# Tile 0 of a fused attention and MLP kernel: two hidden blocks in unsplit float32, normalised rows from the third on, and another order of the first stage

## The chip, the cores and the metric

The kernel runs on one core of one Trainium2 chip. The metric is device time in microseconds (us) of one execution, of which several are taken. Besides, one execution was recorded by the hardware profiler; all durations below come from that one.

The engines are named as in the profile: PE multiplies matrices (PEld loads its weights), DVE is the vector engine, ACT the scalar engine, POOL is GpSimd, and SP only issues DMAs here.

## What is computed

Linear attention with a decay, then an RMS norm with a gated MLP, then a second MLP:

```python
state = alpha[:, :, t, :, None] * state + np.einsum('bhd,bhe->bhde', k[:, :, t], v[:, :, t])
y[:, :, t] = np.einsum('bhd,bhde->bhe', q[:, :, t], state)
...
xn = x / rms * rms_g                    # x: 3072 tokens x 384, rms over the 384
g, val = xn @ w_gate, xn @ w_val        # 384 x 1536 each
x = (g / (1 + exp(-g)) * val) @ w_out   # 1536 x 384
...
h = x @ w_in                            # 384 x 2048
out = (h * cos(h)) @ w_out2             # 2048 x 384
```

All data is float32. There are 4 batches of 8 heads of width 48, over 768 positions.

## The kernel before

**Tiles and units.** The 3072 tokens are 8 tiles of 384 (half a batch each). The attention of a tile is four units, one for a pair of heads: unit 0 to 3 belong to tile 0, unit 4 to 7 to tile 1, and so on; u8 below is the first of tile 2. Features lie on the partitions, tokens along a row.

**A unit** goes through these steps. `att_prep` (L340): DVE scans the decay along the tokens (L347), takes a reciprocal and a second scan (L349), multiplies q (L359) and k (L356). `att_T` (L386): PE transposes k (`pt`), ACT copies it (`th`, L394). `att_sc0` (L424): PE forms the scores (`ps`), ACT copies them and POOL sets the part above the diagonal to zero (`sm`, L398 and L399). `att_u` (L440): PE multiplies k by v (`pu`), DVE scales it (`w`, L454) and adds up the states (L458); what goes on to the next tile is the carry `c`. `att_y` (L474): PE adds scores times v and states times q (`py`), and the sum is copied into the tile's rows `xT`, for tile 0 one half by ACT (L502) and one by DVE (L503). The first unit of a tile holds the pair of heads whose rows fill the 16 spare partitions of the three row blocks, so six small DMAs on SP (`att_fix`, L505: 16 rows each, two to a block) move them there.

**The first MLP** has 12 hidden blocks f of 128. For each: `m1_gate` (L740) forms `pg`, multiplies it by 1/rms (L747, for tiles below NRAW = 3; DVE) and takes Silu on ACT (`th`, L749); `m1_val` (L754) forms `pv`, multiplies it by `th` (L762) and splits the product into `hh` and `hl`; `m1_unit` (L766) adds its three products to the accumulators `o`. After block 11 `o` is scaled, for tile 0 to 2 by 1/rms as well (L779). A float32 matrix is used as the sum of two float32r parts, high and low; `mm9` (L699) multiplies high by high, high by low, low by high: three passes for each block of 128 rows, so nine for `pg` and `pv` and nine for the three `o`.

**The weights** come as float32 seen as 64-bit integers, in pieces of 128 by 768. `assemble` (L183) turns a staged piece (`st_g`, `st_v`, `st_o`; `ws` for later, smaller ones) into floats: the low word on ACT (L186), the high word on ACT (L188), both joined on DVE (`cv`, L189). `split` (L193) makes the two float32r parts: a copy on ACT (L86) and a subtraction on DVE (L89).

**The norm of tile 0.** `x_split` (L598) scales the rows by the norm's weights `g_sb` and splits them; `square` (L516) squares `xT` in three pieces; `rms_rows` (L538) sums them by 12 matmuls; `rms_inv` (L548) finds the inverse root by nine small DVE operations, the last of which spreads it out (`yb`); `rms_out` (L570) turns it into a tile `y0` of all 128 rows by one matmul (`rb`) and an ACT copy (L578).

**Order.** For tile 0 the string FIRST (L48) lists the pieces in the order in which they are issued, and `in_order()` keeps each engine to it: p, T, s, u, y are the steps of a unit, a and b the two halves of a weight's conversion, x, q, r, n, o the norm, g, v, P the first gate and value blocks, S the staging of weights, and i fills PE's time with that many matmuls on ones (`keep_clock`, L531). From there on the pieces of the next tile's attention, and the remaining conversions (steps in CONV, L52), are streamed in by `slot()` (L1038) between the MLP's matmuls; a scheduler in the compiler places the rest. Each engine runs its instructions in that order and waits at the first one that is not ready. SP issues all loads, in one queue, in the order of its list.

Of the kernel before, what the change touches and what calls it, by code (L numbers as in the profile page):

```python
# [55 lines left out]
def fused_kernel(ctx: ExitStack, tc: tile.TileContext, akq, vin, wg, wv, wo, g_in, w2i, w2o, out):  # L56
# [18 lines left out]
    sd = []  # L75

    def make_bd():
        for i in range(1):
            bd.append([at.tile([R, NB, 2, C], F32R, name=f"bd{x}{i}") for x in "hl"])
# [19 lines left out]
    mean = const.tile([128, 128], F32, name="mean")  # L99
    d1 = const.tile([R, NB, C + 1], F32, name="d1")  # L100
# [81 lines left out]

    def assemble(st, v):  # L183
        w = st.bitcast(I32).rearrange("p (n t) -> p n t", t=2)
        lo, hi = w[:, :, 0], w[:, :, 1]
        act.activation(out=lo, in_=lo.bitcast(U32), func=AF.Identity, scale=LOW_SCALE, bias=low)  # L186
        g = hi.bitcast(F32)
        done("act", act.activation(out=g, in_=g, func=AF.Prelu, scale=HIGH_SCALE, alpha=NEG_SCALE))  # L188
# [11 lines left out]
    half = []  # L200

    def conv_a():
# [4 lines left out]
        v = cv_tile(st)  # L207
        assemble(st, v)
        half.append((h, l, v))
        if tag and tag != "ws":  # L210
            free.append(tag)

    def conv_b():
        if half:
            h, l, v = half.pop(0)
            split(h, l, v.bitcast(F32))

# [122 lines left out]
    def att_prep(u):  # L340
        s = un[u]
        a, q = s["a"], s["q"]
        G = at.tile([R, NB, C + 1], F32, tag="G", name="G")
        n = NB * (C + 1)
        Gf = G.rearrange("p n c -> p (n c)")
        Iv = a[:, 1:n + 1]
        dve.tensor_tensor_scan(Gf, a[:, 0:n], d1.rearrange("p n c -> p (n c)"), 0.0, ALU.mult, ALU.add)  # L347
        dve.reciprocal(dr[:, :, C:C + 1], G[:, :, C:C + 1])
        dve.tensor_tensor_scan(  # L349
            Iv[:, ::-1], Iv[:, ::-1], dr.rearrange("p n c -> p (n c)")[:, ::-1],  # L350
            0.0, ALU.mult, ALU.add,
        )
# [86 lines left out]

    def att_u(u):  # L440
# [11 lines left out]
        w = at.tile([R, NB, D], F32, tag="w", bufs=2, name="w")  # L452
# [21 lines left out]
    def att_y(u):  # L474
# [63 lines left out]
    def rms_rows(i, c, n):  # L538
        if i not in rsum:
            rsum[i] = ps_a.tile([128, 512], F32, tag="a", name="rm")  # L540
        x = rms[i][c]
        for j in range(4):
            done("pe", pe.matmul(
                rsum[i][32 * j:32 * j + 32, :TQ], ones[:, :32], x[:, j * TQ:(j + 1) * TQ],
                start=c == 0, stop=c == n - 1,
            ))

    def rms_inv(i):  # L548
        ps = rsum.pop(i)
        m, y, t = (m1.tile([128, TQ], F32, tag="n" + x, name="n" + x) for x in "myt")  # L550
        done("act", act.activation(out=m, in_=ps[:, :TQ], func=AF.Identity, scale=1.0 / DM, bias=eps))
# [29 lines left out]
    def rms_wide(i):  # L581
# [3 lines left out]
        y = at.tile([128, TT], F32, tag="y2", name="y2") if i == 2 else m1.tile([128, TT], F32, tag="y", name="y")  # L585
        t = at.tile([128, TT], F32, tag="nt", name="nt")
# [5 lines left out]
        dve.tensor_tensor(out=t, in0=y, in1=y, op=ALU.mult)  # L592
        dve.tensor_tensor(out=t, in0=t, in1=m, op=ALU.mult)
        for o, s, x, z in (a, ROOT[1], t, t), (y, ROOT[2], a, y), (t, ROOT[3], t, t), (y, ROOT[4], t, y):
            done("dve", dve.scalar_tensor_tensor(out=o, in0=x, scalar=s, in1=z, op0=ALU.add, op1=ALU.mult))
        rms[i] = y

    def x_split(c, i=0):  # L598
        if c == 0:
            xn[i] = tuple(m1.tile([128, 3, TT], F32R, tag="x" + k, name="x" + k) for k in "hl")  # L600
        x, (xh, xl), g = xT[i][:, c, :], xn[i], g_sb[:, c:c + 1]
        ah = act.activation(out=xh[:, c, :], in_=x, func=AF.Copy, scale=g)
        ad = dve.scalar_tensor_tensor(
            out=xl[:, c, :], in0=x, scalar=g, in1=xh[:, c, :].bitcast(F32), op0=ALU.mult, op1=ALU.subtract
        )
        if i == 0:
            done("act", ah)
            done("dve", ad)
# [15 lines left out]
    def att_pieces(i):  # L624
        u0 = 4 * i

        def y(u):
# [4 lines left out]
            if i == 0 and u == u0:  # L632
                att_fix(i)
# [5 lines left out]
        if i == 0:  # L639
            def stage_rest(n):  # L640
# [5 lines left out]
                x=x_split, q=lambda c: square(0, c), r=lambda c: rms_rows(0, c, 3), i=lambda n: keep_clock(n, ones), l=load_all, S=stage_rest, P=lambda f: post.append(m1_gate(0, f)),  # L646
# [52 lines left out]
    def mm9(dst, w, rhs, first, last, cols, mm=pe.matmul):  # L699
        k = 0  # L700
        for kc in range(len(rhs)):
            for a, b in ((0, 0), (0, 1), (1, 0)):
                mm(  # L703
                    dst, w[a][:, cols(kc)], rhs[kc][b],
                    start=first and k == 0, stop=last and k == 3 * len(rhs) - 1,
                )
                k += 1
# [32 lines left out]
    def m1_gate(i, f):  # L740
# [5 lines left out]
        if i < NRAW:  # L746
# [7 lines left out]
    def m1_val(i, f, t):  # L754
# [5 lines left out]
        hh = m1.tile([128, TT], F32R, tag="hh", bufs=3, name="hh")  # L760
        hl = m1.tile([128, TT], F32R, tag="hl", bufs=3, name="hl")
# [4 lines left out]
    def m1_unit(i, f, j, mm=None):  # L766
        g, c = divmod(f, 4)
        if j == 0 and f == 0:
            acc1[i] = [ps_o.tile([128, 512], F32, tag=f"o{n}", name=f"o{n}") for n in range(3)]
        w = wt[f"o{g}"][0]  # L770
        h = hid1[i, f]
        k = slice(c * DM + j * 128, c * DM + j * 128 + 128)
        mm9(acc1[i][j][:, :TT], w, [h], f == 0, f == 11, lambda kc: k, mm or pe.matmul)
        if f == 11:
# [3 lines left out]
            if i < NRAW:  # L778
# [215 lines left out]

    dve.memset(d1, 0.0)
# [3 lines left out]
    dve.memset(eps, EPS)  # L999
# [38 lines left out]
    def slot():  # L1038
# [31 lines left out]
    for i in range(NTILE):  # L1070
# [7 lines left out]
        for f in range(12):  # L1078
# [5 lines left out]
            if f == 0 and 1 <= i < NRAW:  # L1084
                for x in range(2):
                    pre["g", x] = m1_mm(i, "g", x, ps_g.tile([128, 512], F32, tag="g", name="pg"))
                    late.pop(0)()
                    if x == 0:
                        pre["v", 0] = m1_mm(i, "v", 0, ps_g.tile([128, 512], F32, tag="g", name="pv"))
# [119 lines left out]
```

## Time and profile before

| | before |
|---|---|
| median of 3 runs | 994.01 us (993.57 to 994.18) |
| the profiled execution, own time | 995.94 us |
| its span (first to last recorded instruction) | 994.2 us |
| PE busy | 977.3 us, 98% |
| DVE, ACT, POOL busy | 709.5, 608.5, 118.1 us |
| mean granted clock of TensorE | 0.997 of full speed |

The span of the profiled execution is 1.74 us shorter than its own time, and that time is 1.93 us over the median of the runs. A granted clock of 1.00 stands for TensorE's upper level (2.4 GHz), 0.50 for the lower one (1.2 GHz). A row of a timeline that ends in brackets tells how long the engine was idle before it, and which instruction ended the wait.

### The profile page before, as it was taken

The numbers are of one execution on the slowest core, as the hardware profiler recorded it, in microseconds if no ns is written. First come the engines' busy times: TensorE is split into PE (matmuls) and PEld (weight loads), VectorE is DVE, ScalarE is ACT, GpSimd is POOL, SyncE is SP. The second block draws the span as 40 slices with busy tenths as digits, with TensorE's granted clock in tenths as the row PEclk, the third lists the DMA queues.
The fourth block names the chain that finished last, engine by engine and source line by source line (L and its number), as shares of the span: only waits on it lengthen the run. The fifth ranks groups of instructions, "written<-read, shape, count | busy, mean of one in ns | idle before, by whom it ended". The sixth has DMA issues, their size and how long they took to land.

```text
span 994.2 us, 16986 instructions
## 1 busy us (share of the span) xinstructions
PE 977.3 (98%) x6451; PEld 900.9 (91%) x6451; DVE 709.5 (71%) x1333; ACT 608.5 (61%) x1270; POOL 118.1 (12%) x154
## 2 busy tenths in 40 slices
PE   8899999999999999999999999999999999999998
PEld 6698899999999999999999998888888888888886
DVE  7898778978877678578637227777767777777666
ACT  4878455565564565465633227777777677777764
POOL 3010011100110010010102211121201201211000
PEclk9999999999999999999999999999999999999999
DMA  7936334443453443544202575001010010000000
GB/s 232 323 103 193 98 91 128 138 130 96 139 155 101 139 126 102 146 137 126 89 18 88 199 304 170 19 26 39 1 43 22 1 54 12 32 1 1 33 1 32
DMA packets 44273, 96.71 MB, mean 97 GB/s; under 512 B 5520, under 2 KB 25488, under 8 KB 44192
## 3 DMA queue, kind: packets, MB, share of 16 engines
q1 hardware_dynamic: 41312, 79.90, 26.1%
q0 software_dynamic: 2880, 15.73, 4.3%
q8 instruction: 51, 0.84, 0.4%
q14 instruction: 30, 0.25, 0.1%
HBM read 69.26 MB, written 25.17 MB: 95 GB/s over the span
## 4 chain that ended last, share of the span: by engine, by line
PE 91%; DVE 5%; DMA 2%; ACT 1%; issue 1%; POOL 0%; SPq 0%; DVEq 0%; ACTq 0%; POOLq 0%
PE p L841 20%; PE pg L703 14%; PE pv L703 13%; PE o L703 13%; PE px L841 9%; PE py L841 9%; PE py L481 2%; PE pe L841 2%; PE py L486 2%; PE pu L448 1%; DMA ak<-akq 1%; PE ps L382 1%; PE pt L392 1%; PE ps L383 1%; PE ps L384 1%
## 5 line engine op out<-in xcount | busy, mean ns | idle before, releaser
L841 DVE SCALAR_TENSOR_TENSOR kk<-kk,c 128x512 f32<-128x512 int32 x192 | 148.5, 773 | 93.2 <-ACT kk L841 93.2
L841 PE MATMUL p<-hh,p 128*128 128x512 f32 x576 | 211.4, 396 | 0.2 <-ACT kk L841 0.2
L841 PEld LDWEIGHTS p<-hh,p 128*128 128x128 f32 x576 | 108.6, 189 | 17.2 <-ACT kk L841 0.3
L841 ACT ACTIVATE kk<-kk 128x512 f32<-128x512 f32 x192 | 115.7, 626 | 3.0
L841 PE MATMUL p<-hl,p 128*128 128x512 f32 x288 | 113.6, 394 | 0.2 <-DVE hl L89 0.2
L841 PE MATMUL px<-xh,i 128*128 128x256 f32 x481 | 113.8, 291 | 0.0
L841 PE MATMUL py<-xh,i 128*128 128x256 f32 x482 | 109.4, 282 | 0.0
L399 POOL TENSOR_SCALAR_AFFINE_SELECT sm<-sm 128x512 f32<-128x512 f32 (+1 forms) x64 | 46.5, 730 | 455.3 <-ACT sm L398 455.3
L762 DVE TENSOR_TENSOR pv<-th,pv 128x384 f32<-128x384 f32 x96 | 53.3, 556 | 63.3 <-PE pv L703 53.7
L841 PEld LDWEIGHTS px<-xh,i 128*128 128x128 f32 x481 | 84.1, 188 | 12.3 <-ACT py L841 12.3
L86 ACT ACTIVATE hh<-pv 128x384 fp32r<-128x384 f32 x96 | 46.8, 488 | 74.8 <-DVE pv L762 72.7
L841 PEld LDWEIGHTS py<-xh,i 128*128 128x128 f32 x482 | 84.2, 189 | 4.4 <-DVE hl L89 0.3
L749 ACT ACTIVATE th<-pg 128x384 f32<-128x384 f32 x96 | 46.7, 487 | 66.4 <-PE pg L703 45.2
L89 DVE TENSOR_TENSOR hl<-kk,hh 128x512 fp32r<-128x512 f32 x96 | 68.2, 710 | 3.3
L841 PE MATMUL px<-xl,i 128*128 128x256 f32 x240 | 67.8, 283 | 0.0
L841 PE MATMUL py<-xl,i 128*128 128x256 f32 x240 | 67.5, 281 | 0.0
L89 DVE TENSOR_TENSOR hl<-pv,hh 128x384 fp32r<-128x384 f32 x96 | 53.1, 553 | 19.3 <-ACT hh L86 18.3
L841 ACT ACTIVATE kk<-c 128x512 int32<-128x512 f32 x96 | 60.3, 628 | 1.6
L841 PEld LDWEIGHTS p<-hl,p 128*128 128x128 f32 x288 | 54.4, 189 | 5.6 <-DVE hl L89 1.0
L841 ACT ACTIVATE m<-pe 128x256 f32<-128x256 f32 x48 | 18.4, 384 | 53.8 <-PE pe L841 53.8
L841 PEld LDWEIGHTS py<-xl,i 128*128 128x128 f32 x240 | 45.2, 188 | 4.3
L841 ACT ACTIVATE c<-px 128x512 f32<-128x512 f32 x48 | 28.8, 599 | 31.8 <-PE px L841 31.6
(233 smaller groups left out, 2625.8 us busy)
## 6 DMA issues: line engine op xcount, KB each, us to landing
ak<-akq SPq DMA_DIRECT2D x29, 337.8 KB, 3.7
i<-d_i POOLq DMA_DIRECT2D x12, 768.0 KB, 5.9
ws<-w2i SPq DMA_DIRECT2D x16, 384.0 KB, 3.6
ws<-w2o SPq DMA_DIRECT2D x16, 384.0 KB, 3.6
d_p<-whl SPq DMA_DIRECT2D x32, 192.0 KB, 3.0
p<-d_p POOLq DMA_DIRECT2D x8, 768.0 KB, 6.4
v<-vin SPq DMA_DIRECT2D x32, 168.0 KB, 3.0
q<-akq SPq DMA_DIRECT2D x30, 168.0 KB, 2.9
```

The source lines that it names most:

```text
L86: return act.activation(out=dst, in_=src, func=AF.Copy)
L89: return eng.tensor_tensor(out=dst, in0=a, in1=h.bitcast(F32), op=ALU.subtract)
L382: pe.matmul(dst, a[0], b[0], start=start, stop=False)
L383: pe.matmul(dst, a[0], b[1], start=False, stop=False)
L384: pe.matmul(dst, a[1], b[0], start=False, stop=stop)
L399: pool.affine_select(out=dst, in_=dst, pattern=[[0, n], [1, C]], compare_op=ALU.is_ge, fill=0.0, base=0, channel_multiplier=-1,)
L481: pe.matmul(py[r0:r1, c], s["v"][:, n, r0:r1], s["s"][:, n, j, :], start=n == 0, stop=False)
L486: done("pe", pe.matmul(py[:R, c], sd[0][:, n, :], s["q"][:, c], start=False, stop=n == NB - 1))
L703: mm(dst, w[a][:, cols(kc)], rhs[kc][b], start=first and k == 0, stop=last and k == 3 * len(rhs) - 1,)
L749: done("act", act.activation(out=t, in_=p, func=AF.Silu, scale=1.0 / WS))
L762: dve.tensor_tensor(out=p, in0=t, in1=p, op=ALU.mult)
L841: last2[eng] = fn(*args, **kw).ins
```

## The change

The change touches tile 0, the start of tile 1 and the loads ahead of them.

- Hidden blocks 0 and 1 of tile 0 use the weights before they are split ("whole"), against the rows before the norm: three float32 matmuls where nine float32r ones stood, for `pg`, for `pv` and for `o`. `pg` and `pv` are then multiplied by `y0`. The splits of these three pieces are made later (steps 9, 11 and 13 of the stream). From block 2 on, tile 0 uses rows already multiplied by `y0` (`x_norm`), so neither its `pg` nor its `o` is multiplied by it.
- The rows are scaled by `g_sb` when they are copied out of PSUM (for the first unit by `g3`, its own piece of these weights, loaded by six DMAs of 16 values on ACT's queue); the squares are taken from PSUM, unit by unit, so that there are four pieces and 16 matmuls to sum them. For units 0 and 1 ACT copies all 112 rows.
- The low words of the first five weight pieces go to POOL. The high words move ahead (`H`).
- The carries of tile 0 are added up at the end of the list (`C0`). The inverse root takes eight operations, not nine. 23 matmuls on ones remain of 32 issued.
- The key block of unit 1 is loaded ahead of unit 0's v. The DMAs of `att_fix` for row blocks 1 and 2 are issued after unit 0's `y`, those for block 0 after unit 1's.
- At the start of tile 1: `pg` of block 0, the norm, then `pv` of block 0 and `pg` of block 1 in this order.

```diff
 FIRST = (
-    "p0 T0 s0 i4 p1 u0 i5 p2 T1 s1 y0 S4 u1 p3 T2 s2 a0 y1 u2 T3 s3 u3 b0 a1 y2 y3 i7 x0 x1 x2 b1 g0 "
-    "q0 q1 q2 r0 r1 r2 n0 a2 a3 v0 g1 o0 P0 b2 v1 P1 b3"
+    "p0 T0 s0 i4 p1 u0 i3 T1 s1 p2 y0 q0 S4 u1 T2 s2 p3 y1 H0 L0 u2 T3 s3 a0 u3 H0 L0 y2 a1 q1 y3 L0 q2 H0 "
+    "q3 L0 H0 a2 g0 r0 r1 r2 r3 a3 n0 v0 b2 b3 L0 H0 g1 o0 P0 v1 X0 x0 x1 x2 M0 P1 M1 a4 C0"
 )
-CONV = {0, 1, 4, 6, 8, 10, 12, 14} | set(range(16, 36))
+CONV = {1, 4, 6, 8, 10, 12, 14} | set(range(16, 36))
...
+    def conv_low():
+        st = staged[len(lows)][2]
+        lo = st.bitcast(I32).rearrange("p (n t) -> p n t", t=2)[:, :, 0]
+        done("pool", pool.tensor_scalar(
+            out=lo, in0=lo.bitcast(U32), scalar1=LOW_SCALE, scalar2=LOW_BIAS, op0=ALU.mult, op1=ALU.add
+        ))
+        lows.append(st)
...
+            if n == 2 and i == 0:
+                carried.append((p, st[-1], s["ge"], w))
+                continue
...
-            done("act", act.activation(out=x[0:D, p, :], in_=py[0:D, :TT], func=AF.Copy))
-            done("dve", dve.tensor_copy(out=x[64:R, p, :], in_=py[64:R, :TT]))
+            if u < 2:
+                scale = g3[:R] if u == 0 else g_sb[:R, p:p + 1]
+                done("act", act.activation(out=x[:R, p, :], in_=py[:R, :TT], func=AF.Copy, scale=scale))
+            else:
...
+    def square_raw(u):
+        t = m1.tile([128, TT], F32, tag="t" if u else "y", bufs=3 if u else 1, name="sq")
+        done("act", act.activation(out=t[:R], in_=raw.pop(u)[:R, :TT], func=AF.Square))
+        rms.setdefault(0, []).append(t)
...
+    def x_norm():
+        xn[0] = x_pair()
+        for c in range(3):
+            f = m1.tile([128, TT], F32, tag="t", bufs=3, name="xf")
+            done("dve", dve.tensor_tensor(out=f, in0=xT[0][:, c, :], in1=rms[0], op=ALU.mult))
+            done("act", copy_r(xn[0][0][:, c, :], f))
+            x0.append(f)
...
-            if i == 0 and u == u0:
-                att_fix(i)
+            if i == 0 and u < 2:
+                att_fix(i, (1, 2) if u == 0 else (0,))
...
+    def full(i, f):
+        return i == 0 and f < 2
...
+        if full(i, f):
+            w = wt0[a]
+            for kc in range(3):
+                o = c * 384 + kc * 128
+                done("pe", pe.matmul(p[:, :TT], w[:, o:o + 128], xT[0][:, kc, :], start=kc == 0, stop=kc == 2))
+            return p
...
-        if i < NRAW:
+        if raw_tile(i) or full(i, f):
             done("dve", dve.tensor_tensor(out=p, in0=p, in1=rms[i], op=ALU.mult))
...
-    for u in range(4):
-        load_all(u)
+    for c in range(3):
+        for r in (0, 64):
+            act.dma_start(out=g3[r + 16 * c:r + 16 * c + 16], in_=g_in[r + 48:r + 64, c:c + 1])
+    att_load(0)
+    att_loadq(0)
+    att_load(1)
+    att_loadv(0)
+    att_loadq(1)
+    att_loadv(1)
     sp.dma_start(out=g_sb, in_=g_in)
+    load_all(2)
+    load_all(3)
...
+        if step[0] in (9, 11, 13):
+            with behind():
+                conv_whole()
```

How the rows of an engine's list move is seen at three places. The first is SP, from the first stage's weights on (`xT` are the DMAs of `att_fix`, `ak` and `q` the loads for unit 4). Before:

```order
14 L128 DMA st_v_162<-wv 128x768
15 L508 DMA xT<-xT 16x384
16 L509 DMA xT<-xT 16x384
17 L508 DMA xT<-xT 16x384
18 L509 DMA xT<-xT 16x384
19 L508 DMA xT<-xT 16x384
20 L509 DMA xT<-xT 16x384
21 L128 DMA st_g_268<-wg 128x768
22 L128 DMA st_v_270<-wv 128x768
23 L128 DMA st_o_274<-wo 128x768
24 L128 DMA st_o_276<-wo 128x768
25 L314 DMA ak<-akq 112x772
```

and changed:

```order
14 L130 DMA st_v_170<-wv 128x768
15 L579 DMA xT<-xT 16x384
16 L580 DMA xT<-xT 16x384
17 L579 DMA xT<-xT 16x384
18 L580 DMA xT<-xT 16x384
19 L130 DMA st_g_272<-wg 128x768
20 L130 DMA st_v_274<-wv 128x768
21 L130 DMA st_o_278<-wo 128x768
22 L130 DMA st_o_280<-wo 128x768
23 L579 DMA xT<-xT 16x384
24 L580 DMA xT<-xT 16x384
25 L351 DMA ak<-akq 112x772
```

Four weight pieces now stand ahead of the last two DMAs of `att_fix`, those of row block 0. The second place is PE where the attention of tile 0 ends and the MLP begins. Before:

```order
63 L490 MATMUL py<-akq,w 48x128 x4
64 L534 MATMUL idle<-ones 128x128 x7
65 L703 MATMUL pg<-xh,g0h 128x384
...
73 L703 MATMUL pg<-xh,g0l 128x384
74 L543 MATMUL rm<-sq,ones 32x96 x12
75 L703 MATMUL pv<-xh,v0h 128x384
```

and changed:

```order
63 L545 MATMUL py<-akq,w 48x128 x4
64 L826 MATMUL pg<-xT,whole 128x384 x3
65 L615 MATMUL rm<-sq,ones 32x96 x16
66 L826 MATMUL pv<-xT,whole 128x384 x3
67 L826 MATMUL pg<-xT,whole 128x384 x3
68 L648 MATMUL rb<-yb,ones 128x384
69 L826 MATMUL pv<-xT,whole 128x384 x3
70 L794 MATMUL pg<-xh,g0h 128x384 x3
```

The matmuls on ones are gone from here, and the first float32r weights are used at the third `pg`. The third place is DVE from the last `xT` copy to the root, in the changed kernel (`ny`, `nt` are the root; `whole` and `cv` the joined words of a weight piece):

```order
37 L564 TENSOR_SCALAR xT<-py,g_sb 48x384
38 L217 SCALAR_TENSOR_TENSOR whole<-st_v_170 128x768
39 L564 TENSOR_SCALAR xT<-py,g_sb 48x384
40 L217 SCALAR_TENSOR_TENSOR cv<-st_g_272 128x768
41 L217 SCALAR_TENSOR_TENSOR cv<-st_v_274 128x768
42 L633 TENSOR_SCALAR ny<-nm 128x96
```

Three joins now stand between the states of unit 3 and the root, each of which needs a low word from POOL; before, the first two pieces were joined and split there, with their low words from ACT.

## Rows read from the trace of the kernel before

**Rows 1.** Busy time of each engine, with its share and instructions.
```profile
PE 977.3 (98%) x6451; PEld 900.9 (91%) x6451; DVE 709.5 (71%) x1333; ACT 608.5 (61%) x1270; POOL 118.1 (12%) x154
```

**Rows 2.** Stretches: length; PE, PEld, DVE, ACT, POOL busy; clock; DMA share; GB/s.
```profile
21.45:24.86 3.41, 3.41 (x40) 2.69 (x36) 3.21 (x9) 3.17 (x7) 0.99 (x2) 0.50 0.89 350
27.95:57.00 29.05, 24.75 (x155) 20.77 (x153) 26.25 (x48) 25.25 (x42) 0.52 (x1) 1.00 0.80 272
57.00:90.20 33.20, 33.13 (x243) 30.27 (x242) 29.00 (x55) 25.99 (x54) 3.04 (x5) 1.00 0.48 140
90.20:93.10 2.90, 1.13 (x13) 0.72 (x14) 2.90 (x7) 2.84 (x8) 0.00 (x0) 1.00 0.33 73
93.10:96.50 3.40, 3.40 (x33) 2.69 (x29) 3.40 (x9) 2.96 (x7) 0.00 (x0) 0.50 0.54 170
```

**Rows 3.** Timeline of PE from unit 3 to the norm: start, duration, what.
```profile
20.45 0.48 PE L392 MATMUL pt<-ident,akq 112*128 112x112 f32 x3 [1.11 <-issue]
...
26.36 1.83 PE L534 MATMUL idle<-ones 128*128 128x128 f32 x14
27.95 0.42 PE L703 MATMUL pg<-xh,g0h 128*128 128x384 f32 x1
...
29.95 0.94 PE L543 MATMUL rm<-sq,ones 128*32 128x96 f32 x24
...
34.34 0.91 PE L573 MATMUL rb<-yb,ones 128*128 128x384 f32 x2
```

**Rows 4.** Timeline of DVE, units 1 to 3, then the spreading of the root.
```profile
8.00 0.96 DVE L347 TENSOR_TENSOR_SCAN G<-ak,d 112x387 f32<-112x387 f32 x1 [1.09 <-ACT th L394]
...
12.46 0.96 DVE L347 TENSOR_TENSOR_SCAN G<-akq,d 112x387 f32<-112x387 f32 x1
...
15.71 0.56 DVE L503 COPY xT<-py 48x384 f32<-48x384 f32 x1
...
16.95 0.27 DVE L458 SCALAR_TENSOR_TENSOR c<-w,ge 112x48 f32<-112x48 f32 x1
17.14 0.96 DVE L347 TENSOR_TENSOR_SCAN G<-akq,d 112x387 f32<-112x387 f32 x1
...
33.73 0.56 DVE L564 SCALAR_TENSOR_TENSOR yb<-ny,rsel 128x384 f32<-128x384 f32 x1
```

**Rows 5.** DMA issues at 2.7, 5.0, 15.1, 19.2 and 21.0 us: KB, us to landing.
```profile
ak<-akq SPq DMA_DIRECT2D x1, 337.8 KB, 5.2
akq<-akq SPq DMA_DIRECT2D x1, 505.8 KB, 9.4
xT<-xT SPq DMA_DIRECT2D x1, 24.0 KB, 4.0
xT<-xT SPq DMA_DIRECT2D x1, 24.0 KB, 1.9
st_o<-wo SPq DMA_DIRECT2D x1, 768.0 KB, 8.7
```

**Rows 6.** Timeline of SP, the first issue behind the six `xT` DMAs.
```profile
19.89 0.58 SPq L128 DMA_DIRECT2D st_g<-wg  x1
```

**Rows 7.** Timeline of PE at 241 us: an unsplit float32 matmul, 128 rows by 384.
```profile
241.17 0.81 PE L584 MATMUL rm<-sq,mean 128*128 128x384 f32 x2
```

**Rows 8.** Chain that ended last, 57 to 92 us: start, duration, what.
```profile
73.33 1.58 PE pg L703 x9
...
82.69 5.91 DMA ak<-akq
```

**Rows 9.** DVE by line and shape, 0 to 125 us: count, busy, mean ns.
```profile
L747 DVE TENSOR_TENSOR pg<-pg,y 128x384 f32<-128x384 f32 x14 | 7.7, 558 | 0.2 <-PE pg L703 0.2
```

**Rows 10.** The same of POOL, whole span: one input, then two.
```profile
L399 POOL TENSOR_SCALAR_AFFINE_SELECT sm<-sm 128x384 f32<-128x384 f32 x16 | 10.1, 643 | 91.0 <-ACT sm L398 91.0
...
L89 POOL TENSOR_TENSOR xl<-x,xh 128x512 fp32r<-128x512 f32 x10 | 13.0, 1300 | 71.8 <-ACT xh L841 71.8
```

**Rows 11.** DMA issue at 6.6 us, on SP: KB, us to landing.
```profile
g_sb<-gin SPq DMA_DIRECT2D x1, 1.5 KB, 8.3
```

More of the change, by code (lines that the diff above doesn't have):

```diff
@@ L75, in fused_kernel @@
     sd = []
+    yn = []
     def make_bd():
         for i in range(1):
-            bd.append([at.tile([R, NB, 2, C], F32R, name=f"bd{x}{i}") for x in "hl"])
+            bd.append([at.tile([R, NB, 2, C], F32R, tag=f"bd{x}", name=f"bd{x}{i}") for x in "hl"])
             for t in bd[-1]:
@@ L181, in in_order, with conv_high, high_first @@
             yield
+    lows = []
+    def conv_low():
[5 more added lines that the diff above has]
+        lows.append(st)
+    highs = []
+    def conv_high(st):
+        g = st.bitcast(F32).rearrange("p (n t) -> p n t", t=2)[:, :, 1]
+        done("act", act.activation(out=g, in_=g, func=AF.Prelu, scale=HIGH_SCALE, alpha=NEG_SCALE))
+    def high_first():
+        st = staged[len(highs)][2]
+        conv_high(st)
+        highs.append(st)
     def assemble(st, v):
@@ L185, in assemble @@
         lo, hi = w[:, :, 0], w[:, :, 1]
-        act.activation(out=lo, in_=lo.bitcast(U32), func=AF.Identity, scale=LOW_SCALE, bias=low)
-        g = hi.bitcast(F32)
-        done("act", act.activation(out=g, in_=g, func=AF.Prelu, scale=HIGH_SCALE, alpha=NEG_SCALE))
+        if lows and lows[0] is st:
+            lows.pop(0)
+        else:
+            act.activation(out=lo, in_=lo.bitcast(U32), func=AF.Identity, scale=LOW_SCALE, bias=low)
+        if st in highs:
+            highs.remove(st)
+        else:
+            conv_high(st)
         done("dve", dve.scalar_tensor_tensor(
@@ L200, in fused_kernel @@
     half = []
+    whole = []
+    wt0 = {}
     def conv_a():
@@ L206, in conv_a @@
         h, l = (x[:, o:o + st.shape[-1]] for x in wt[key][0])
-        v = cv_tile(st)
+        first = key[1] == "0" and o == 0
+        v = at.tile([128, 768], I32, tag=dict(g="bdh", v="bdl", o="yn")[key[0]], name="whole") if first else cv_tile(st)
+        if first:
+            wt0[key[0]] = v.bitcast(F32)
         assemble(st, v)
-        half.append((h, l, v))
+        (whole if first else half).append((h, l, v))
         if tag and tag != "ws":
@@ L216, in conv_b, with conv_whole @@
             split(h, l, v.bitcast(F32))
+    def conv_whole():
+        h, l, v = whole.pop(0)
+        split(h, l, v.bitcast(F32))
     def conv_piece():
@@ L355, in att_prep @@
         q3 = q.rearrange("p (n c) -> p n c", c=C)
-        dve.tensor_tensor(out=k3, in0=k3, in1=Iv.rearrange("p (n c) -> p n c", c=C + 1)[:, :, 1:], op=ALU.mult)
-        ge = at.tile([R, NB, 1], F32, tag="ge", bufs=3, name="ge")
+        if u >= 4:
+            dve.tensor_tensor(out=k3, in0=k3, in1=Iv.rearrange("p (n c) -> p n c", c=C + 1)[:, :, 1:], op=ALU.mult)
+        ge = at.tile([R, NB, 1], F32, tag="ge" if u >= 4 else "ge0", bufs=3 if u >= 4 else 4, name="ge")
         done("act", copy_r(ge, G[:, :, C:C + 1]))
-        done("dve", dve.tensor_tensor(out=q3, in0=q3, in1=G[:, :, 1:], op=ALU.mult))
+        ins = dve.tensor_tensor(out=q3, in0=q3, in1=G[:, :, 1:], op=ALU.mult)
+        if u < 4:
+            ins = dve.tensor_tensor(
+                out=k3, in0=k3, in1=Iv.rearrange("p (n c) -> p n c", c=C + 1)[:, :, 1:], op=ALU.mult
+            )
+        done("dve", ins)
         s.update(ge=ge, k=k, q=q)
@@ L402, in causal @@
         )
+        done("pool", ins)
     def att_sm(u):
@@ L438, in att_sc0, with carry_on @@
             causal(sm[:, :, j, :], ps[:, :TT].rearrange("p (n c) -> p n c", c=C), NB)
+    carried = []
+    def carry_on():
+        for p, x, ge, w in carried:
+            done("dve", dve.scalar_tensor_tensor(
+                out=carry[p], in0=x, scalar=ge[:, 2, :], in1=w[:, 2], op0=ALU.mult, op1=ALU.add
+            ))
     def att_u(u):
@@ L541, in rms_rows, with root @@
         x = rms[i][c]
+        k = 128 if i else R
         for j in range(4):
             done("pe", pe.matmul(
-                rsum[i][32 * j:32 * j + 32, :TQ], ones[:, :32], x[:, j * TQ:(j + 1) * TQ],
+                rsum[i][32 * j:32 * j + 32, :TQ], ones[:k, :32], x[:k, j * TQ:(j + 1) * TQ],
                 start=c == 0, stop=c == n - 1,
             ))
+    def root(m, y, t, a):
+        dve.tensor_tensor(out=t, in0=y, in1=y, op=ALU.mult)
+        dve.tensor_tensor(out=t, in0=t, in1=m, op=ALU.mult)
+        for o, s, x, z in (a, ROOT[1], t, t), (y, ROOT[2], a, y), (t, ROOT[3], t, t), (y, ROOT[4], t, y):
+            done("dve", dve.scalar_tensor_tensor(out=o, in0=x, scalar=s, in1=z, op0=ALU.add, op1=ALU.mult))
     def rms_inv(i):
@@ L591, in rms_wide, with x_pair @@
         )
[L592 to L595, printed above, removed]
+        root(m, y, t, a)
         rms[i] = y
+    x0 = []
+    def x_pair():
+        return tuple(m1.tile([128, 3, TT], F32R, tag="x" + k, name="x" + k) for k in "hl")
+    def x_norm():
[5 more added lines that the diff above has]
+            x0.append(f)
     def x_split(c, i=0):
+        if i == 0:
+            xh, xl = xn[0]
+            done("dve", sub_r(dve, xl[:, c, :], x0[c], xh[:, c, :]))
+            return
         if c == 0:
-            xn[i] = tuple(m1.tile([128, 3, TT], F32R, tag="x" + k, name="x" + k) for k in "hl")
+            xn[i] = x_pair()
         x, (xh, xl), g = xT[i][:, c, :], xn[i], g_sb[:, c:c + 1]
-        ah = act.activation(out=xh[:, c, :], in_=x, func=AF.Copy, scale=g)
-        ad = dve.scalar_tensor_tensor(
+        act.activation(out=xh[:, c, :], in_=x, func=AF.Copy, scale=g)
+        dve.scalar_tensor_tensor(
             out=xl[:, c, :], in0=x, scalar=g, in1=xh[:, c, :].bitcast(F32), op0=ALU.mult, op1=ALU.subtract
         )
-        if i == 0:
-            done("act", ah)
-            done("dve", ad)
     def xn_write(i):
@@ L696, in att_pieces, with mm9 @@
         return L
[L699 to L707, printed above, removed]
+    def mm9(dst, w, rhs, first, last, cols, mm=pe.matmul, low_last=False):
+        terms = [(kc, a, b) for kc in range(len(rhs)) for a, b in ((0, 0), (0, 1), (1, 0))]
+        if low_last:
+            terms.sort(key=lambda x: (x[2], x[1], x[0]))
+        for k, (kc, a, b) in enumerate(terms):
+            mm(dst, w[a][:, cols(kc)], rhs[kc][b], start=first and k == 0, stop=last and k == len(terms) - 1)
     hid1 = {}
@@ L760, in m1_val @@
         hh = m1.tile([128, TT], F32R, tag="hh", bufs=3, name="hh")
+        if full(i, f):
+            done("dve", dve.tensor_tensor(out=p, in0=p, in1=rms[i], op=ALU.mult))
+            done("dve", dve.tensor_tensor(out=hh.bitcast(F32), in0=t, in1=p, op=ALU.mult))
+            hid1[i, f] = hh.bitcast(F32)
+            return
         hl = m1.tile([128, TT], F32R, tag="hl", bufs=3, name="hl")
@@ L767, in m1_unit @@
         g, c = divmod(f, 4)
-        if j == 0 and f == 0:
+        start, stop = f == 0, f == 11
+        if j == 0 and start:
             acc1[i] = [ps_o.tile([128, 512], F32, tag=f"o{n}", name=f"o{n}") for n in range(3)]
-        w = wt[f"o{g}"][0]
+        w = parts_w(f"o{g}", f)
         h = hid1[i, f]
         k = slice(c * DM + j * 128, c * DM + j * 128 + 128)
-        mm9(acc1[i][j][:, :TT], w, [h], f == 0, f == 11, lambda kc: k, mm or pe.matmul)
-        if f == 11:
+        if full(i, f):
+            pe.matmul(acc1[i][j][:, :TT], wt0["o"][:, k], h, start=start, stop=stop)
+        else:
+            mm9(acc1[i][j][:, :TT], w, [h], start, stop, lambda kc: k, mm or pe.matmul)
+        if stop:
             o = m1.tile([128, TT], F32, tag="t", bufs=3, name="x2")
@@ L788, in m1_out @@
             m1_unit(i, f, j)
-        if f == 11 and i < NRAW:
+        if f == 11 and raw_tile(i):
             rms.pop(i)
@@ L1084, in fused_kernel @@
             if f == 0 and 1 <= i < NRAW:
[L1085 to L1089, printed above, removed]
+                pre["g", 0] = m1_mm(i, "g", 0, ps_g.tile([128, 512], F32, tag="g", name="pg"))
+                late.pop(0)()
+                with tc.issue_after(mark["pe"]):
+                    pre["v", 0] = m1_mm(i, "v", 0, ps_g.tile([128, 512], F32, tag="g", name="pv"))
+                    pre["g", 1] = m1_mm(i, "g", 1, ps_g.tile([128, 512], F32, tag="g", name="pg"))
+                late.pop(0)()
             t = post.pop(0) if post else m1_gate(i, f)
             slot()
-            m1_val(i, f, t)
+            if (i, f) not in hid1:
+                m1_val(i, f, t)
             if last and f % 4 == 3:
```

51 lines of the change are left out of this document (33 added, 18 removed).

## The prediction, made before the changed kernel ran

> **What bounds the kernel now.** I read the busy times first: PE is busy for 977.3 of 994.2 us [rows 1], so outside a few stretches only fewer or faster matmuls would count. The view by stretches shows where that is not so [rows 2]. From 28 to 57 us PE works for 24.75 of 29.05 us, while DVE is busy for 26.25 and ACT for 25.25: here tile 0 waits for conversions and gates. From 57 to 90.2 us PE is full (33.13 of 33.20). From 90.2 to 93.1 us it works for only 1.13 of 2.90 us, and in the 3.40 us behind that its granted clock is 0.50, the lower level. The same happens earlier: ahead of unit 3's transposes PE waits 1.11 us [rows 3], and from 21.45 to 24.86 us the clock is 0.50 [rows 2]. In both places the clock fell just after PE had stood idle and come back. What can be won lies in three places, then: the time until the first weight matmul (27.95 us, [rows 3]), the stretch to 57 us, and the gap at 90 us with its slow clock (1.77 us idle, and half of 3.40, that is 1.70: together 3.47).
>
> **The attention of tile 0.** DVE sets its pace: the first scans of units 1, 2 and 3 start at 8.00, 12.46 and 17.14 us [rows 4].
> - *Unit 1.* Its key block is issued at 2.67 us and lands 5.2 later, at 7.87 [rows 5]. From there to 14.43, where unit 3's block lands (5.03 + 9.4), SP's queue brings 505.8 KB twice and 168 KB three times, 1516 KB in 6.56 us or 231 KB per us. Unit 0's v, 168 KB, no longer lies ahead: 0.73 us. Scan at 7.2, 0.8 earlier.
> - *Unit 2.* By DVE's own pace 4.46 us later, less a carry (0.2): 11.5. Its block, behind 842 KB, lands at 7.87 + 3.64 = 11.5 as before. I take 11.65.
> - *Unit 3.* The step took 4.68 us; the `xT` copy (15.71, 0.56) and the carry (16.95, 0.2 with the pause to the scan) leave it [rows 4]: 3.9, so 15.5, 1.65 earlier. Its block has landed. Its transposes go from 20.45 to 18.8.
> - *The end of `py`.* It was at 26.4, where the matmuls on ones begin [rows 3]: 24.75 by the shift alone, 23.1 if the 3.41 us of slow clock go too. I take 23.7.
>
> **The first weight matmul** needs row block 0, whose two small DMAs now stand behind four weight pieces (3.1 MB) on SP. How such a queue acts is in the rows: a 24 KB copy issued at 15.1 us, behind two weight pieces, landed after 4.0, one issued at 19.2 in an emptied queue after 1.9 [rows 5]. Before, the four pieces were issued from 19.89 us [rows 6], and one of the last two, issued at 20.99, took 8.7, to 29.7: that is 1.9 until the first bytes and 7.9 of flow. Now they are issued at about 17.5 (two DMAs fewer ahead, the copy they wait for earlier), but the first stage's pieces hold the path until 19.1, so the flow ends at 27.0 at the latest, and at about 26.4 if, as I take it, part of the four moves while the path drains. First weight matmul: 26.6, **1.35 us earlier**. Its bounds are 23.8 (the small copies don't wait; -4.1) and 27.6 (issue at 17.5 and 9.8 as before, and their own end; -0.35).
>
> That leaves PE idle from 23.7 to 26.6, with nothing to fill it, where before matmuls on ones ran right up to the weights [rows 3]. So I expect one more stretch at the lower clock. It could cost half of 3.4, 1.7; as the clock fell only 1.0 us after the return at 20.45 [rows 2, 3] and not all that follows waits for PE, I take **1.2 us lost** (bounds 0 and 1.7).
>
> **From there to 57 us.** The nine matmuls of a `pg` take 1.58 us, 0.175 each [rows 8]. An unsplit one shows 0.81 from start to end [rows 7]; as a split one of 0.34 follows the next after 0.175, I take 0.65. So 54 split ones out and 18 unsplit in make 11.7 - 9.45 = 2.25 us more, and 16 instead of 12 sums 0.3 more (24 records take 0.94, [rows 3]): 2.6 us, inside the 4.3 that PE is idle here [rows 2]. The norm comes later against the first matmul: `pg` 1.95, sums 1.25, `pv` and `pg` 3.9 stand ahead of `rb`, which ends after another 0.91, so 8.0 behind the first weight matmul, where it was 34.34 + 0.91 - 27.95 = 7.3 [rows 3]. The root itself is not what waits: one operation shorter than the one that ended in `yb` at 34.29 [rows 4], it is done while PE still multiplies. Against these 0.7 us stand three DVE subtractions that move behind 57 us and five low words that leave ACT; DVE and ACT bound this stretch. I let the two cancel: the 1.35 survive.
>
> **POOL's five low words** have no row. The nearest: one input, 128x384, 0.643 us, for 768 columns 1.3; two inputs, 128x512, 1.300, for 768 columns 1.95 [rows 10]. A low word has one input, but reads every second word and converts integers: I take 1.5, between them (0.64, the first row unscaled, is the lower end, 3.9, twice the two-input one, the upper). The joins of the first four stand ahead of the root on DVE. The first starts at about 18.3 (an estimate: unit 2's masks are done a little ahead of unit 3's transposes), unit 3's masks (2 x 0.643) come between, so the fourth ends at 19.6 + 4P and its join about 1 us later (DVE takes 0.56 for 384 columns, [rows 9]); the root can start at 26.6 + 1.95 + 1.25 + 0.4 = 30.2. Up to P = 2.4 they cost nothing. The Trainium skill speaks against this part: "GPSIMD Engine Reference", "Engine selection", puts elementwise work on the vector engine, with GpSimd about half as fast on two inputs and near its pace on one. By its one-input case P stays near the row's 1.3, and the sum is the same; only by its two-input case, on a vector-engine price of 1 us, would it be 2, still without cost.
>
> **The gap at 90 us.** It begins with DVE: the scan of unit 8 waits for its key block, issued at 82.69 us and landed 5.91 later [rows 8], and a gate's multiplication stands behind it. That block will come no earlier. But behind 57 us DVE has less to do: eight more of tile 0's gates come without the multiplication by `y0` (0.56 each, [rows 9]), 4.5 us, against three subtractions moved there (about 1 us each): 1.5 us less, and two gates and two copies (some 2 us) less ahead of 57 us, where the carries (4 x 0.27, [rows 4]) are only moved. That is about as much as PE's 1.77 us idle, or more. Then the gates are ahead of PE and the gap closes: **3.5 us won**, with it the slow clock. Bounds 0 and 3.5.
>
> **Sum.** -1.35 + 1.2 - 3.5 = -3.65. The profiled execution took 995.94 us, so 992.3 there; the median of the runs, 994.01, is 1.93 lower, so **990.4**. All else keeps its order on a full PE, and stays.
>
> **The rivals.**
> - *The gap stays* (0.20). PE comes to tile 1's first gates no later than before, DVE still meets the wait with a multiplication behind it, and the clock falls. For it: the block's issue waits for PE and stands behind weight loads as before. Against it: DVE's 1.5 to 3 us. Time: -0.15, 993.9; 992.7 if the clock at 24 to 30 us holds up.
> - *The six small DMAs on ACT are late* (0.10). ACT's copy of unit 0's decay sums stands behind the last, which waits for an earlier one; an `xT` copy took 1.9, `g_sb`'s 1.5 KB behind SP's loads 8.3 [rows 5, 11]. At 8.3 ACT would be held until about 11.5 us, and unit 1's scan with it, some 4.5 us; DMA waits on SP go with it. Up to about 3.6 it costs nothing. Time: 994.9; 998 if two such landings stand one behind the other. The Trainium skill ("DMA: Bandwidth & Descriptors", "Queues, rings and completion order") has each DMA engine alternate between queues packet by packet, by which ACT's copies wouldn't wait for SP's bytes; no run here shows it yet.
> - *Slower: POOL's low words* (0.12). Beyond P = 2.4 each us costs four, since the root waits for the fourth join, and at P = 3.3 the whole gain is gone. At 3.9 it is 6.0 - 3.65 = 2.35 slower: 996.4. For it: five operations of a kind that POOL has not run here; against: nothing that POOL does on 512 columns takes more than 1.3.
>
> **How the numbers follow.** What a measurement of this kernel tells from no change is about 0.2%, 2 us: below 992.0 is faster, above 996.0 slower. The forecast has 0.58, all of it faster; the first rival (0.20) and 0.06 of the second lie within 2 us; 0.04 of the second and the third (0.12) are slower. So faster 0.58, same 0.26, slower 0.16. The range: without a loss of clock 989.2, with block 0 at 23.8 as well 986.4, so 986.2 at the lower end; above, the first two rivals and the start of the third, 996.0. The forecast's own range is 986.2 to 992.
>
> **What would show it.** Right: DVE's scans at about 7.2, 11.65 and 15.5 us; the first `pg` at 26.6, just after the block-0 copies land; granted clock 0.50 once between 26 and 31 us; low words on POOL of 1.3 to 2 us; unit 8's scan still waiting for `ak`, but PE without idle time around 90 us and no clock of 0.50 there. Wrong: idle PE before 57 us growing beyond 4.3 us after the first `pg`, DVE waiting for POOL ahead of the root, ACT's first copy later than 9 us, or the gap at tile 1 again.

## The result, and the profile after

The change made the kernel slower: 1002.02 us (median of 6 runs, 1001.22 to 1003.98) against 994.10 for the kernel before in the same comparison (6 runs). The ratio is 1.0083, with a 95% interval of 1.007 to 1.0096. The forecast was 990.4 us, its range 986.2 to 996.0, and 0.16 stood on slower, on other mechanisms than the one that came. The profiled execution took 1002.33 us and has a span of 1000.3.

The busy times barely moved (against [rows 1]):

```profile
PE 980.3 (98%) x6423; PEld 898.9 (90%) x6423; DVE 704.3 (70%) x1321; ACT 606.1 (61%) x1266; POOL 125.9 (13%) x159
```

The timeline of PE, from the end of tile 0's attention to the matmul of the norm, answers to [rows 3]:

```profile
23.07 0.64 PE L545 MATMUL py<-akq,w 48*48 48x128 f32 x8
29.99 4.18 PE L826 MATMUL pg<-xT,whole 128*128 128x384 f32 x6 [6.28 <-DMA xT<-xT]
34.09 1.51 PE L615 MATMUL rm<-sq,ones 112*32 112x96 f32 x32
35.53 2.27 PE L826 MATMUL pv<-xT,whole 128*128 128x384 f32 x6
37.64 2.10 PE L826 MATMUL pg<-xT,whole 128*128 128x384 f32 x6
39.57 0.81 PE L648 MATMUL rb<-yb,ones 128*128 128x384 f32 x2
```

The attention ends at 23.71 us, where 23.7 had been forecast. Then PE waits 6.28 us for the DMAs of row block 0; the first `pg` starts at 29.99 us, 2.04 later than before and not 1.35 earlier. Its three matmuls take 4.18 us where the next `pg` takes 2.10, and `rb` starts 5.2 us later than in [rows 3]. The view by stretches shows why the first ones take twice as long (columns as in [rows 2]): the granted clock is 0.50, the lower level, until the end of the sums.

```profile
31.00:35.00 4.00, 4.00 (x29) 2.01 (x32) 0.00 (x0) 0.00 (x0) 0.00 (x0) 0.50 1.02 350
35.00:41.00 6.00, 6.00 (x33) 3.60 (x26) 4.03 (x11) 3.09 (x5) 0.00 (x0) 0.94 0.88 303
41.00:57.00 16.00, 13.96 (x60) 10.02 (x58) 15.83 (x31) 13.04 (x23) 0.00 (x0) 1.00 0.51 171
57.00:90.00 33.00, 32.74 (x235) 29.70 (x235) 30.64 (x57) 27.41 (x53) 5.40 (x6) 1.00 0.36 104
```

In the first of these four stretches DVE, ACT and POOL do nothing at all: everything waits for `pg` and the sums behind it.

The DMA rows, against [rows 5] (KB, us from issue to landing): the last of the four weight pieces, issued at 19.28 us, and the two copies for row block 0 that are queued behind it, issued at 19.7 and 20.3 us.

```profile
st_o<-wo SPq DMA_DIRECT2D x1, 768.0 KB, 10.1
...
xT<-xT SPq DMA_DIRECT2D x1, 24.0 KB, 9.9
...
xT<-xT SPq DMA_DIRECT2D x1, 24.0 KB, 9.6
```

24 KB took 9.9 us, where the same copy took 1.9 in an emptied queue [rows 5].

The scans of DVE start at 7.04, 11.84 and 15.75 us (forecast 7.2, 11.65, 15.5), and `yb` is spread at 37.99:

```profile
7.04 0.96 DVE L384 TENSOR_TENSOR_SCAN G<-ak,d 112x387 f32<-112x387 f32 x1 [0.34 <-DMA ak<-akq]
...
11.84 0.96 DVE L384 TENSOR_TENSOR_SCAN G<-akq,d 112x387 f32<-112x387 f32 x1 [0.90 <-DMA akq<-akq]
...
15.75 0.96 DVE L384 TENSOR_TENSOR_SCAN G<-akq,d 112x387 f32<-112x387 f32 x1
...
36.04 0.21 DVE L633 TENSOR_SCALAR ny<-nm 128x96 int32<-128x96 int32 x1 [7.75 <-ACT nm L630]
...
37.99 0.56 DVE L639 SCALAR_TENSOR_TENSOR yb<-ny,rsel 128x384 f32<-128x384 f32 x1
```

At tile 1 the gap of [rows 2] at 90 us has become one wait without a slow clock, later in the program (timeline of PE; `w` is the scaled k times v of `att_u`):

```profile
107.36 0.82 PE L479 MATMUL ps<-q,ak 48*128 48x128 f32 x5 [1.47 <-DVE w L506]
```

### The profile page after: what moved, and what is told of

Its sections match the earlier page's. It is cut to its first block, busy times and chain, and to the rows that moved or that the text cites. A ratio compares the mean times of both kernels' runs of the same rounds, so it can differ in the third digit from the quotient of the medians.

```text
span 1000.3 us, 16937 instructions
## 1 busy us (share of the span) xinstructions
PE 980.3 (98%) x6423; PEld 898.9 (90%) x6423; DVE 704.3 (70%) x1321; ACT 606.1 (61%) x1266; POOL 125.9 (13%) x159
## 4 chain that ended last, share of the span: by engine, by line
PE 90%; DVE 2%; DMA 1%; ACT 0%; issue 0%; ACTq 0%; DVEq 0%
PE p L952 20%; PE pv L794 14%; PE pg L794 14%; PE o L794 14%; PE px L952 9%; PE py L952 9%; PE py L536 2%; PE pe L952 2%; PE py L541 2%; PE pu L500 1%; DMA d_i<-whl 1%; PE ps L425 1%; PE ps L427 1%; PE ps L426 1%; PE ps L479 1%; PE pt L435 1%
## 5 line engine op out<-in xcount | busy, mean ns | idle before, releaser
L442 POOL TENSOR_SCALAR_AFFINE_SELECT sm<-sm 128x512 f32<-128x512 f32 (+1 forms) x64 | 49.3, 775 | 416.7 <-ACT sm L441 416.6
```

The lines of the kernel that those rows point to most:

```text
L442: ins = pool.affine_select(out=dst, in_=dst, pattern=[[0, n], [1, C]], compare_op=ALU.is_ge, fill=0.0, base=0, channel_multiplier=-1,)
```

## The experiments

Theory A: the late row block 0 is the loss, with the slow clock behind its wait. Theory B: the two float32 blocks and the later norm are. Theory C came with the first results: behind `y0` DVE is the bound. All runs below were timed beside the kernel before, whose median was 994.4 to 994.6 there.

**e1, block 0 first.** `S4`, which stages the four pieces, stands behind `y1`, and waits for both copies of block 0:

```diff
-    ... p2 y0 q0 S4 u1 T2 s2 p3 y1 H0 ...
+    ... p2 y0 q0 u1 T2 s2 p3 y1 S4 H0 ...
```

> The changed kernel with one thing different: the two DMAs of att_fix for row block 0 are issued ahead of the four weight pieces (S4 stands behind y1 in FIRST), so that only SP's list changes. Theory A, the late block 0 is the loss: the copies land about 2 us after their issue near 19 us, the first pg starts at about 23.8 instead of 29.99 us, without a stretch at half clock behind it; the root then waits for the fourth join (about 28.5), y0 is copied at about 33 instead of 40.91 us, and the time falls by 7 to 8 us, to 994 to 995. Theory B, the two float32 blocks and the norm that comes later are the loss, and the wait for block 0 only hides part of it: the time falls by less than 4 us and stays above 998. If the whole of the wait is won and the other gains of the change are real as well (the gap at 90 us gone), 992 or less.

Measured: 995.14 us, ratio 1.001 (0.9996 to 1.0024). The copies land 2.5 us after the last issue. Timeline of PE:

```profile
22.84 2.39 PE L826 MATMUL pg<-xT,whole 128*128 128x384 f32 x6
25.16 0.87 PE L615 MATMUL rm<-sq,ones 112*32 112x96 f32 x32
25.95 2.20 PE L826 MATMUL pv<-xT,whole 128*128 128x384 f32 x6
27.99 2.10 PE L826 MATMUL pg<-xT,whole 128*128 128x384 f32 x6
31.48 0.91 PE L648 MATMUL rb<-yb,ones 128*128 128x384 f32 x2 [1.39 <-DVE yb L639]
```

`pg` follows `py` without a pause, the clock is 1.00, and `rb` comes 8.1 us earlier than in the changed kernel (0.8 of it because the attention ended earlier in this recorded execution). PE's list is the same in both; 100 us into the program e1 is 8.3 us ahead, at the end 8.6, and the medians differ by 6.9, against two medians of the kernel before that differ by 0.3. So the place of two 24 KB copies in SP's queue makes 6.9 of the 7.9 us that the change lost: theory A. Theory B would have left it above 998.

**e2, the same delay alone, in the kernel before.** `att_fix` is split as in the change, all else is as before:

```diff
-            if i == 0 and u == u0:
-                att_fix(i)
+            if i == 0 and u < 2:
+                att_fix(i, (1, 2) if u == 0 else (0,))
```

> The kernel before with one thing different: att_fix's DMAs for row block 0 follow unit 1's y, behind the four weight pieces, as in the change; the lists of PE and all other engines stay. Theory A: the first weight matmul moves from 27.95 to about 29.5 to 30 us, PE stands idle for 1.5 to 2 us behind the matmuls on ones; 996 if the clock holds, up to 998 if it falls to 0.50 for some 3.4 us. Theory B: the copies are hidden as before, 994 within 1 us.

Measured: 1000.15 us, ratio 1.0059 (1.0037 to 1.0081). The row of the first weight matmul:

```profile
31.36 0.69 PE L703 MATMUL pg<-xh,g0h 128*128 128x384 f32 x1 [3.92 <-ACT xh L602]
```

It comes 3.4 us later than in [rows 3], and the clock is at 0.50 from 31 to 37 us. The releaser named is ACT's scaling of the rows (`xh`), which itself waits for block 0. Theory A on its own ground, and more than I expected, as the last of the four pieces took 10.3 us to land.

**e3, the wait filled.** 24 matmuls on ones ahead of the first weight matmul of the changed kernel:

```diff
-    ... H0 a2 g0 r0 ...
+    ... H0 a2 i9 i9 i6 g0 r0 ...
```

> The changed kernel with 24 matmuls on ones (about 6.3 us) between the end of the attention of tile 0 and the first weight matmul, so that PE is not idle while block 0 is awaited; nothing else is moved. If the slow clock behind that wait costs what its rows say (pg 4.18 us for 2.10 at full clock, the sums 1.51), the granted clock stays at 1.00, the first pg starts at 30 us as before, y0 comes 2 to 2.5 us earlier and the time falls by as much, to 999.5 to 1000. Rival: what follows is bound by DVE and ACT, so that a faster pg changes nothing: 1001.5 to 1002.

Measured: 1003.28 us, ratio 1.0089 (1.006 to 1.0117), the changed kernel's own loss. The clock did hold at the first `pg` (2.17 us for its three matmuls, the sums 0.87), and `rb` came 2.2 us earlier. But in the recorded execution it fell behind the next wait, the one of 1.57 us for `g1l`, which ended at 55.06:

```profile
54.00:55.00 1.00, 0.00 (x0) 0.00 (x0) 1.00 (x3) 1.00 (x5) 0.00 (x0) 1.00 0.77 310
...
56.00:57.00 1.00, 1.00 (x4) 0.76 (x3) 1.00 (x2) 1.00 (x2) 0.00 (x0) 0.50 0.00 0
57.00:58.00 1.00, 1.00 (x10) 0.72 (x10) 1.00 (x3) 1.00 (x2) 0.00 (x0) 0.50 0.00 0
58.00:59.00 1.00, 1.00 (x5) 1.00 (x6) 1.00 (x3) 1.00 (x3) 0.74 (x1) 0.50 0.00 0
```

So in that execution the slow clock was moved and not removed, and in the median the expected 2 us did not come. But one of the four executions had a mean granted clock of 1.000 and took 999.72 us, inside the 999.5 to 1000 that were expected; the other three (0.993 to 0.997) took 1002.47 to 1004.90. Nor does such a wait always bring the slow clock: in e1 the same wait of 1.53 us left it at 1.00.

**e4, low words back on ACT.** The five `L0` leave FIRST of the changed kernel.

> The changed kernel with the first five low words back on ACT and none on POOL. If POOL's low words cost nothing (they took 0.86 to 1.45 us each and the last join ahead of the root ended at 28.3 us, long before the sums at 35.6), the time stays within 1.5 us of 1002, or rises a little, as ACT gets 5 us of work back in a stretch where it has to wait in any case. Rival, POOL's work and its contention with DVE slow the start: 1000 or less.

Measured: 1004.38 us, ratio 1.0099 (1.0074 to 1.0123), 0.0016 over the changed kernel's, with intervals that overlap: the low words on POOL did no harm, and may have helped a little.

**e5, e6, e7, e8: where e1 stands still.** All four start from e1. Its DVE has no idle time from 28.3 to 57.5 us; PE waits 1.39 us for its root and 1.53 for `g1l`. e5 moves the fourth join behind the root, e6 takes the fixed order at tile 1 out of e1, e7 puts five subtractions of `split` on POOL, e8 is e5 and e7:

```diff
 e5: -... r3 a3 n0 v0 ...     +... r3 n0 a3 v0 ...
 e7: -            done("dve", sub_r(dve, l, f, h))
     +            done("pool", sub_r(pool, l, f, h))
```

> The kernel of e1 with one more thing different: the join of the fourth weight piece (a3) stands behind the root (n0) in FIRST, not ahead of it. In e1's trace DVE waits 1.72 us for that piece's low word, and PE then waits 1.39 us for yb. Theory C, from y0 on DVE is the bound (it has no idle time from 28.3 to 57.5 us in e1): the root starts near 26.5 us, rb at 30.1 as PE gets free, y0 1.4 us earlier, and the whole program follows: 1.4 us faster than e1, 992.5 to 994 where before has 994.4. Rival: the work that y0 releases waits for weights or ACT instead, and nothing changes.

> The kernel of e1 with the start of tile 1 written as before (pg, pv and the norm left to the scheduler). If the fixed order there is worth what the rows of the wait for rb show (0.43 us before, none in e1), the time is within 1 us of e1; if it is what closed the gap at 90 us or what keeps tile 1 going, it is 2 us or more slower than e1.

> The kernel of e1 with five subtractions of split (g0l and v0l of the fourth block's pieces ahead of y0's use, and the three deferred ones of the whole pieces) on POOL instead of DVE: 5 x 0.95 us less on DVE, about 5 x 1.95 on POOL, which is idle there. Theory C (DVE is the bound from y0 to 57 us): g1l, for which PE waits 1.5 us at 49.5 in e1, ends 1.5 to 2 us earlier, and the time is 1.5 to 3 us under e1's. Rival D: two-input operations on POOL slow DVE's own ones beside them, and POOL's masks for tile 1 come late behind the subtractions: no gain, or slower.

> e5 and e7 together. Theory C: the gains add up, 3 to 4 us under e1, about 991, and under the kernel before by more than 2 us. Rival: PE's own work is the bound once DVE has slack (3.2 us more of it than before, 18 unsplit matmuls at 0.70 for 54 split ones at 0.175), and e8 is no better than the better one of e5 and e7.

Measured: e5 996.28 us (ratio 1.0016, 1.0003 to 1.0029), e6 999.60 (1.0046, 1.0029 to 1.0062), e7 1003.38 (1.0096, 1.0073 to 1.0119), e8 1001.14 (1.0068, 1.0056 to 1.0080). None is faster than e1.

- e5 missed a wait on another engine: on ACT the high word of the same piece still stood ahead of the root's copy and waited for it to land (1.40 us idle); `nm` started at 27.68 us, and `y0` was copied at 33.68 (e1: 32.43), behind a `v0h` for whose join, now later, ACT stood idle for 3.38 us.
- e6: without the fixed order `rb` of tile 1 waits 1.78 us, and the clock falls behind it and once before. The order is worth its place; I had read only 0.43 us from the kernel before.
- e7: rival D, and stronger than I wrote it. Timeline of POOL, then of DVE:

```profile
28.84 1.83 POOL L90 TENSOR_TENSOR g0l<-cv,g0h 128x768 fp32r<-128x768 f32 x1 [1.01 <-ACT g0h L87]
30.63 1.82 POOL L90 TENSOR_TENSOR v0l<-cv,v0h 128x768 fp32r<-128x768 f32 x1
```

```profile
29.03 1.76 DVE L627 TENSOR_TENSOR nt<-ny 128x96 f32<-128x96 f32 x1
30.82 1.74 DVE L628 TENSOR_TENSOR nt<-nt,nm 128x96 f32<-128x96 f32 x1
32.60 0.90 DVE L630 SCALAR_TENSOR_TENSOR nm<-nt 128x96 f32<-128x96 f32 x1
33.53 0.26 DVE L630 SCALAR_TENSOR_TENSOR ny<-nm,ny 128x96 f32<-128x96 f32 x1
```

Each of the first two small DVE operations, 0.26 us each in the changed kernel, lasts until the POOL instruction beside it ends, within 0.2 us. `yb` came 3.5 us later than in e1, PE waited 5.04 us for it, and the clock fell.

**e9, the root ahead of the fourth piece on every engine.** On e1:

```diff
-    "q3 L0 H0 a2 g0 r0 r1 r2 r3 a3 n0 v0 b2 b3 L0 H0 g1 o0 P0 v1 X0 x0 x1 x2 M0 P1 M1 a4 C0"
+    "q3 a2 g0 r0 r1 r2 r3 n0 L0 H0 a3 v0 b2 g1 o0 P0 v1 X0 x0 x1 x2 b3 L0 H0 M0 P1 M1 a4 C0"
```

> The kernel of e1 with the fourth weight piece behind the root on every engine: its low word (POOL), its high word (ACT) and its join (DVE) follow n0 in FIRST, its split of the value weights (b3) and the fifth piece follow x2; PE's list stays. In e5 only the join was moved, and the root's copy nm stayed behind the high word on ACT, which waits for the piece to land (ACT 1.40 us idle, nm at 27.68). Theory C: nm starts at about 26.1, yb is ready before PE gets free at 30.1, rb follows without a wait, y0 is copied at 31 instead of 32.43 us in e1, and the time falls by about 1.4 us against e1 and more where a wait of 1.39 us brought the slow clock: 992 to 993.5. Rival, DVE is already full behind y0 and only the order of its work changes: the same as e1, 995.

Measured: 995.27 us, ratio 1.0007 (0.9994 to 1.0019): the rival. `rb` no longer waits, but a gate does: PE waits 1.38 us for `hh`, and 1.5 for `g1l` as before; DVE is busy for 28.47 of the 29.00 us from 28 to 57 (e1: 28.52). In the recorded execution the clock also fell in the attention, so that the first `pg` came at 24.25.

**e10, two parts in the kernel before.** Six matmuls on ones ahead of unit 3's transposes (`u2 i6 T3`), and the fixed order at tile 1:

> The kernel before with two things of the change's kind: six matmuls on ones ahead of unit 3's transposes (where PE waited 1.11 us and the clock then fell to 0.50 for 3.41 us), and the fixed order at the start of tile 1. If the slow clock between 21 and 25 us delays tile 0 and the order at tile 1 saves its wait of 0.43 us, the time falls by 1 to 2 us against before, to 992.5 to 993.5. Rival, DVE sets the pace in both places (its scans, then its root): within 0.7 us of before.

Measured: 994.12 us, ratio 1.0001 (0.9992 to 1.0011). The rival: nothing was won. No version tried is faster than the kernel before.

## Why the prediction was wrong

The result is 11.6 us above the forecast. By e1 some 6.9 of them come of the late row block 0; the other 4.7 are gains that did not come.

- **The attention, right.** Scans within 0.25 us, the end of `py` at 23.71 for 23.7.
- **The first weight matmul, the step that failed.** I had it at 26.6, with 27.6 as the latest; it was 29.99. The mechanism was in the text (two small copies behind 3.1 MB); the term that was mis-sized is the 7.9 us of flow of the four pieces. They are the flow of three. The piece of [rows 5] that landed at 29.7 is the third of the four; the fourth was issued 0.48 us behind it and took 11.2 (SP's timeline and the DMA row of the kernel before):

```profile
21.47 0.65 SPq L128 DMA_DIRECT2D st_o<-wo  x1
...
st_o<-wo SPq DMA_DIRECT2D x1, 768.0 KB, 11.2
```

It landed at 32.7, so the flow was 10.9 us there. In the forecast's own sum the flow then ends at 19.1 + 10.9 = 30.0 and not at 27.0 at the latest, or at 29.4 with the 0.6 that I took off, and the first `pg` comes 0.2 behind it: a loss of some 1.6 to 2.2 us, not a gain of 1.35. The changed kernel agrees: the four were issued from 16.74 us, the path was held until 19.3, and the last piece landed at 29.3, the copies 0.2 and 0.5 behind it. From the first of the four issues to the last landing it was 12.6 us here, 12.8 in the kernel before, 12.9 in e1 and 12.4 in e2. My upper bound had the same error: its 9.8 us after the issue are those of the third piece.
- **The slow clock, forecast, mis-sized.** I took 1.2 us; the first `pg` lost 2.08 (4.18 against 2.10) and the sums 0.64 (1.51 against 0.87), 2.7 together, as all that followed did wait for PE there. The wait ahead of it was 6.28 us in place of the 2.9 forecast. Whether its length set the loss is not shown: in e3 the clock was at 0.50 from about 55.5 to 62 us behind a wait of 1.57.
- **"I let the two cancel", not so.** An unsplit matmul took 0.70 us, not 0.65, so PE's extra work is 3.15 us and not 2.25. And behind `y0` DVE is full: e1 has `y0` 2.9 us ahead of the kernel before, and by executions with a mean granted clock of 1.000 it is only about half a us faster, 993.3 (three executions) against 993.9 (fifteen of the kernel before, over three comparisons). That e1 is no faster than before speaks against this part of the forecast too. It is not the forecast's kernel in all else, as its four pieces are issued 1.8 us later and DVE waits 1.72 us for the fourth; but e9, whose `rb` waits for nothing, is no faster either. That DVE is the bound there is read from its busy time: no run took work off it without another cost.
- **The gap at 90 us, half right.** It closed and its slow clock went, as forecast; but in its place stands the wait of 1.47 us at 107: DVE waits 1.45 us for unit 8's key block up to 100.08 and is all but full from there on. And the 1.70 us of slow clock were one execution's: the kernel before was recorded 21 times in the last comparison, with granted clocks from 0.996 to 1.000, and e10 has the gap without the slow clock. I priced as certain what seems to happen in some executions only.
- **POOL's low words, right.** 0.86 to 1.45 us each (forecast 1.5), no cost in the changed kernel (e4), where the root waits for PE in any case. In e1 the root comes earlier, and one of its operations lasted 0.84 us in place of 0.26 beside a low word. The Trainium skill, "GPSIMD Engine Reference", "Key points", has GpSimd and the vector engine share their interfaces to SBUF, with contention when a vector instruction has two inputs there; the trace of e7 agrees, with 1.76 us for such an operation of 0.26.
- **The rivals.** The six small DMAs on ACT took 2.6 to 4.5 us while SP's loads were in flight; DVE's scan of unit 1 did not wait for them. The slower side had the wrong mechanism. What came was the forecast's own first term, with a price and bounds read from the wrong one of four pieces.
- What stays open: of its lead on e10 in the recorded executions, 2.5 us at the root of tile 1, e1 keeps 0.5 at the end; part goes in two waits near 350 us (0.74 and 0.29 us), part in small steps in the second MLP, whose order is unchanged. No run was made on that.

## What to carry to other kernels

A small transfer that the critical path awaits belongs ahead of bulk loads in its queue, however small it is: price it by the landing of the last piece ahead of it, and make sure that the row read is that of the last one. Before a stage is made to start earlier, ask which engine is full behind it; there the lead is lost again, and a lead on one engine moves nothing while a neighbour in the same order waits for a load. A slow clock read from one execution is a chance and not a term of a sum, and filling one wait can leave it to the next.

## What was not expected of the hardware

Beside a two-input operation on POOL a DVE operation of 0.26 us lasted 1.76 us, until POOL's instruction ended (e7); and the granted clock, kept at 1.00 by matmuls on ones through the time that block 0 was awaited, fell to 0.50 behind the next wait of 1.57 us in the recorded execution (e3).
